# Four moves in the opening of a one-core attention and GEGLU block: the w_phi load, one x tile, the mask product and one PSUM copy

## The chip, the core and the metric

The kernel runs on one core of one Trainium2 chip. The metric is the device time of one execution in microseconds (us); the time of a version is the median of its runs. The names of the engines follow the profile: PE is TensorE's matmul, PEld its weight load, DVE is VectorE, ACT is ScalarE, POOL is GpSimd, SP is SyncE (here it only issues DMAs), and ACTq and SPq are the instruction queues of ACT and SP, from which DMAs are issued.

## What is computed

A pre-layernorm transformer block over 2048 rows of 640 features, in bf16: linear attention with a learned feature map (32 heads of 20), then a gated feed-forward layer of width 1536.

```python
def _A_ref(x, wqkv, w_phi, wo):
    qkv = (x @ wqkv).reshape(B, S, 3, H, Dh).transpose(2, 0, 3, 1, 4)
    q, k, v = qkv[0], qkv[1], qkv[2]
    pq = jnp.einsum("bhsd,hdf->bhsf", q, w_phi)
    pk = jnp.einsum("bhsd,hdf->bhsf", k, w_phi)
    phi_q = jnp.concatenate([_softmax(pq), _softmax(-pq)], axis=-1)
    phi_k = jnp.concatenate([_softmax(pk), _softmax(-pk)], axis=-1)
    kv = jnp.einsum("bhsf,bhsd->bhfd", phi_k, v)
    z  = jnp.einsum("bhsf->bhf", phi_k)
    num = jnp.einsum("bhqf,bhfd->bhqd", phi_q, kv)
    den = jnp.einsum("bhqf,bhf->bhq", phi_q, z)[..., None] + 1e-6
    return (num / den).transpose(0, 2, 1, 3).reshape(B, S, D) @ wo

def _B_ref(x, w_gate, w_up, w_down):
    return (_gelu(x @ w_gate) * (x @ w_up)) @ w_down

h = x + _A_ref(_layernorm(x), A_wqkv, A_w_phi, A_wo)
h2 = h + _B_ref(_layernorm(h), B_w_gate, B_w_up, B_w_down)
```

## The kernel before

**Tiling.** The 2048 rows are 16 tiles of 128 rows, in four blocks of four (x_sb[0] to x_sb[3]). The 640 features are 5 chunks of 128. Weights stay in SBUF.

**Stages.** (1) An opening, the first 17 us: loads, layernorm of the first six tiles, their transposes, the first V projections, and the fold of w_phi into W_k. (2) For each of 16 tiles a K projection, its exponentials, its normalisation, and the sums over rows (kv_tile). (3) Q projections and the attention output. (4) Gate, up and down projections for four blocks of rows. The change lies in stage 1.

**The fold.** w_phi acts on each head of 20 columns after the K projection. The kernel multiplies it into the weights instead: bd() (line 410) spreads w_phi (128 x 5 x 20) into a block-diagonal matrix BD (128 x 5 x 8 x 20, 800 elements in a partition) by a product with a 0/1 mask hmask, and fold() (line 224) multiplies the transposed W_k (WkT, loaded with transposing DMAs) by BD. A fold goes chunk by chunk, d = 0 to 4: six matmuls into a PSUM tile wa, then one copy of wa into Wk2. The tuple KA (line 48) names the chunks whose copy ACT makes; DVE makes the others. Before the change KA is (0, 1, 2, 4).

**Order.** The instructions of every engine are issued in the order in which the program is written, and each engine runs its own in that order, waiting at each for what it needs. The rows of lines 419 to 460 are that order for stage 1. What matters of it: the layernorm of tiles 0 and 1 is applied in two parts. The mean is subtracted before the transpose (xc, lines 263 and 403); the factor rstd is applied when V is copied out of PSUM (v_ev, line 306). For tile 0, ACT computes rstd. For tile 1, st_act (line 383) has ACT make the two sums and POOL make rstd, with lines 390 (variance plus epsilon), 391 (power -0.5) and 392 (its negative, used later by K). Tiles 2 and 3 have statistics on DVE (line 116, 120), the root on ACT (lines 126, 127) and the normalisation on DVE (ln_ap, line 151); tiles 4 and later have the root on POOL (lines 134, 135).

**PSUM.** All PSUM tiles of stage 1 come from one pool psG of four buffers. A new tile takes the buffer that was given back first, in the order of the program, and its first matmul waits for the copy that empties that buffer. In stage 1 the first fold's wa follows tile 0's V (pv), the second fold's wa follows tile 1's V, and the V projection of tile 3 follows the transpose of tile 3.

**Loads.** SP issues, in this order: x tiles 0, 1 and 2 (160 KB each), W_v's chunks 0 and 1, chunks 2 and 3 (320 KB each), x tile 3, W_v's chunk 4 (160 KB), x tiles 4 and 5 (320 KB), five transposing loads of W_k, and later the rest of x. ACT's queue issues w_phi (25 KB, in rows of 40 bytes), and then the load of an activation table (line 186).

Of the kernel before, what the change touches and what calls it, by code (L numbers as in the profile page):

```python
# [17 lines left out]
def kernel(  # L18
# [12 lines left out]
    nc = tc.nc  # L31
    P = 128
# [3 lines left out]
    Dh = 20  # L36
# [8 lines left out]
    H0 = [(P * c) // Dh for c in range(NC)]  # L45
    NH = [(P * c + P - 1) // Dh - H0[c] + 1 for c in range(NC)]
    VP = (0, 2, 4, 6, 9, 11)
    KA, QA = (0, 1, 2, 4), (0, 1, 2, 3, 4)
    LQ = (7, 8, 9, 9, 10)
    FQ = (10, 11, 12, 13, 14)  # L50

# [19 lines left out]
    x_v = A_x.rearrange("b (p t) d -> p (b t) d", t=NT)  # L71
    o_v = out.rearrange("b (p t) d -> p (b t) d", t=NT)
    w_v = A_wqkv.rearrange("(c p) n -> p c n", p=P)
    phi_v = A_w_phi.rearrange("h d f -> (h d) f")
# [8 lines left out]
    x_sb = [const.tile([P, 4, D], BF16, name=f"x_sb{b}") for b in range(NB)]  # L83
    wphi = const.tile([P, NC, Dh], BF16, name="wphi")
# [9 lines left out]
    BD = const.tile([P, NC, 8, Dh], BF16, name="BD")  # L94
# [86 lines left out]
    nc.gpsimd.memset(nhalf, -0.5)  # L181
    nc.gpsimd.memset(eps, EPS)
    nc.sync.dma_start(x_sb[0][:, 0:1, :], x_v[:, 0:1, :])
    nc.sync.dma_start(x_sb[0][:, 1:2, :], x_v[:, 1:2, :])
    nc.scalar.dma_start(wphi, phi_v.rearrange("(c p) f -> p c f", p=P))
    nc.scalar.add_instruction(mybir.InstLoadActFuncSet(name=nc.get_next_instruction_name(), act_func_set_id=6))
    nc.sync.dma_start(x_sb[0][:, 2:3, :], x_v[:, 2:3, :])
    nc.sync.dma_start(Wv[:, 0:2, :], w_v[:, 0:2, 2 * D:3 * D])
    nc.sync.dma_start(Wv[:, 2:4, :], w_v[:, 2:4, 2 * D:3 * D])
    nc.sync.dma_start(x_sb[0][:, 3:4, :], x_v[:, 3:4, :])  # L190
    nc.sync.dma_start(Wv[:, 4:5, :], w_v[:, 4:5, 2 * D:3 * D])
    nc.sync.dma_start(x_sb[1][:, 0:2, :], x_v[:, 4:6, :])

    def load_T(WT, i, *ds):
# [215 lines left out]
    def bd(c0, c1):  # L410

        n = c1 - c0
        nc.vector.tensor_tensor(BD[:, c0:c1], wphi[:, c0:c1, None, :].to_broadcast([P, n, 8, Dh]),
                                hmask[:, c0:c1, :, None].to_broadcast([P, n, 8, Dh]), ALU.mult)

    def tr_c(t):
# [6 lines left out]
    tr_c(1)  # L423
    ln_st(2, act=False, log=True)
    bd(0, NC)
    st_act(1, 1)
    warm(*[P] * 4)
# [430 lines left out]
```

## Time and profile before

| what | us |
|---|---|
| three runs | 275.83, 274.81, 275.75 |
| median | 275.75 |
| profiled execution, its own time | 275.48 |
| its span in the profile | 273.4 |
| PE busy (share of the span) | 268.0 (98%) |
| DVE, ACT, POOL busy | 174.5, 141.1, 96.0 |

The granted TensorE clock is 1.00 throughout. By stretches of the opening, from the busy time of each engine in given windows:

| window, us | PE | PEld | DVE | ACT | POOL | DMA share |
|---|---|---|---|---|---|---|
| 0 to 6 | 5.11 | 3.09 | 2.70 | 3.15 | 3.07 | 0.64 |
| 6 to 12 | 5.13 | 3.85 | 5.38 | 3.88 | 1.19 | 0.99 |
| 12 to 18 | 6.00 | 4.78 | 5.02 | 5.07 | 2.02 | 0.93 |
| 18 to 24 | 6.00 | 4.30 | 5.88 | 5.78 | 4.52 | 0.31 |

The first 4 us of PE are warm-up matmuls on constants (line 222), which produce nothing that is used. In a timeline row the numbers ahead of the engine are start and duration; the bracket behind a row gives how long the engine had been idle and what ended that. Rows on POOL are rough.

### The profile page before, as it was taken

How to read it: one execution, taken by the hardware profiler on the slowest of the kernel's cores; microseconds unless marked ns; L12 is line 12 of the kernel's file. 1: busy time of each engine (PE TensorE's matmuls, PEld its weight loads, DVE VectorE, ACT ScalarE, POOL GpSimd, SP SyncE). 2: the span in 40 equal slices, each digit the busy share in tenths (PEclk: the TensorE clock that was granted, in tenths of full speed). 3: DMA queues.
4: the chain of work that ended last, by engine and by line, in shares of the span. 5: the costliest groups of instructions: out<-in, count | busy, mean ns of one | idle time of the engine just before them, and what ended most of it. 6: DMA issues, size and time to landing. Idle time of an engine off the chain costs nothing.

```text
span 273.4 us, 7242 instructions
## 1 busy us (share of the span) xinstructions
PE 268.0 (98%) x2983; PEld 172.0 (63%) x3000; DVE 174.5 (64%) x332; ACT 141.1 (52%) x241; POOL 96.0 (35%) x220
## 2 busy tenths in 40 slices
PE   7999999999999999999999999999999999999996
PEld 4777767775555887788755555675555576444574
DVE  5889999997675866685459864336966333333332
ACT  5789897887799765364524445213354500223100
POOL 4248888775102226374221552101165300000000
PEclk9999999999999999999999999999999999999999
DMA  6972557670698022323202235210414111000011
GB/s 193 208 250 51 65 62 98 75 162 13 223 368 278 4 50 50 74 55 70 48 27 52 26 70 47 51 50 1 74 29 70 25 48 50 24 0 0 2 48 48
DMA packets 42400, 21.46 MB, mean 78 GB/s; under 512 B 35200, under 2 KB 40576, under 8 KB 42368
## 3 DMA queue, kind: packets, MB, share of 16 engines
q1 hardware_dynamic: 41712, 20.98, 33.9%
q8 instruction: 23, 0.38, 0.6%
q10 hardware_dynamic: 656, 0.03, 0.2%
q14 instruction: 9, 0.07, 0.1%
HBM read 10.18 MB, written 2.62 MB: 47 GB/s over the span
## 4 chain that ended last, share of the span: by engine, by line
PE 94%; DMA 3%; ACT 1%; issue 1%; DVE 1%; SPq 0%
PE gu L694 38%; PE pd L713 19%; PE po L634 8%; PE pq L376 8%; PE pk L287 7%; PE pv L287 6%; PE ab L562 2%; PE kvp L354 2%; DMA Wv<-in_A_wqkv_dram 2%; DMA LN1T<-ln 2%; PE wa L240 1%; PE tp L159 1%; PE pv L303 1%; ACT vS L307 1%; DVE LN1T L160 0%
## 5 line engine op out<-in xcount | busy, mean ns | idle before, releaser
L700 DVE TENSOR_TENSOR GT<-gu,g 128x512 bf16<-128x512 f32 (+1 forms) x60 | 34.5, 581 | 47.3 <-PE gu L694 38.5
L697 ACT ACTIVATE g<-gu 128x512 bf16<-128x512 f32 (+1 forms) x60 | 30.8, 513 | 63.5 <-PE gu L694 63.4
L694 PE MATMUL gu<-LN2T,Wg 128*128 128x512 bf16 (+1 forms) x289 | 61.2, 335 | 0.6
L694 PE MATMUL gu<-LN2T,Wu 128*128 128x512 bf16 (+1 forms) x300 | 61.8, 336 | 0.0
L713 PE MATMUL pd<-Wd,GT 128*128 128x320 bf16 (+2 forms) x396 | 53.5, 295 | 0.0
L713 PEld LDWEIGHTS <-GT 128*128 128x128 bf16 x396 | 37.9, 98 | 14.6 <-DVE GT L700 0.2
L694 PEld LDWEIGHTS <-Wu 128*128 128x128 bf16 x300 | 29.3, 98 | 22.6
L694 PEld LDWEIGHTS <-Wg 128*128 128x128 bf16 x300 | 28.6, 98 | 20.8
L287 PEld LDWEIGHTS <-LN1T 128*128 128x128 bf16 x290 | 27.7, 98 | 10.8 <-DMA LN1T<-ln 0.5
L716 DVE TENSOR_TENSOR y<-pd,x_sb 128x320 bf16<-128x320 f32 (+2 forms) x29 | 13.9, 480 | 29.4 <-PE pd L713 29.4
L335 POOL TENSOR_TENSOR vt<-vS,rs 128x672 bf16<-128x672 bf16 x22 | 29.2, 1346 | 8.6 <-DVE rs L331 7.9
L634 PE MATMUL po<-Wo,oT 128*128 128x320 bf16 x160 | 24.4, 299 | 0.0
L287 PE MATMUL pk<-Wk,LN1T 128*128 128x320 bf16 x160 | 24.2, 299 | 0.0
L376 PE MATMUL pq<-LN1T,Wq 128*128 128x512 bf16 x94 | 22.9, 379 | 0.3
L327 DVE TENSOR_REDUCE sk<-E 128x64 f32<-128x1280 bf16 x16 | 22.9, 1430 | 0.0
L381 ACT ACTIVATE Eq<-pq 128x1024 bf16<-128x1024 f32 (+1 forms) x26 | 20.0, 830 | 3.3 <-PE pq L376 3.3
L287 PE MATMUL pv<-Wv,LN1T 128*128 128x320 bf16 x130 | 19.8, 299 | 0.1
L320 ACT ACTIVATE E<-pk 128x640 bf16<-128x640 f32 x28 | 18.3, 708 | 3.2 <-PE pk L287 3.2
L634 PEld LDWEIGHTS <-oT 128*128 128x128 bf16 x160 | 15.5, 98 | 7.0 <-ACT oT L160 0.5
L146 ACT ACTIVATE ln<-x_sb,v,rstd 128x640 bf16<-128x640 bf16 x14 | 12.9, 923 | 10.7 <-POOL v L673 10.3
L611 DVE TENSOR_TENSOR tt<-AB,w 128x1280 bf16<-128x1280 f32 x12 | 17.8, 1485 | 1.0 <-POOL w L604 0.9
L376 PEld LDWEIGHTS <-Wq 128*128 128x128 bf16 x100 | 9.3, 98 | 9.7
(115 smaller groups left out, 289.2 us busy)
## 6 DMA issues: line engine op xcount, KB each, us to landing
out_dram<-y SPq DMA_DIRECT2D x15, 160.0 KB, 1.8
Wg<-in_B_w_gate_dram SPq DMA_DIRECT2D x1, 1920.0 KB, 7.8
Wu<-in_B_w_up_dram SPq DMA_DIRECT2D x1, 1920.0 KB, 8.8
Wd<-in_B_w_down_dram SPq DMA_DIRECT2D x2, 960.0 KB, 12.1
x_sb<-in_A_x_dram SPq DMA_DIRECT2D x2, 640.0 KB, 6.3
Wo<-in_A_wo_dram SPq DMA_DIRECT2D x1, 800.0 KB, 5.4
x_sb<-in_A_x_dram SPq DMA_DIRECT2D x4, 160.0 KB, 3.4
Wv<-in_A_wqkv_dram SPq DMA_DIRECT2D x2, 320.0 KB, 4.7
```

The source lines that it names most:

```text
L287: nc.tensor.matmul(ps[:, u, 0:HD], lhsT=lnT(t, c), rhs=W[:, c, u * HD:(u + 1) * HD], start=(c == 0), stop=(c == NC - 1))
L320: nc.scalar.activation(Ek[t][:, s, :].rearrange("p (u f) -> p u f", u=2), pk[:, :, 0:HD], ACTF.Exp, scale=((lnp[t][2], nrstd[t]) if t in C ...
L327: nc.vector.reduce_sum(sk, Ek[t].rearrange("p s (h f) -> p (s h) f", f=Dh), axis=AX.X)
L335: eng.tensor_tensor(vt[:, s], vS[t % 8], rs[:, s * H:(s + 1) * H, None].to_broadcast([P, H, VC]), ALU.mult)
L376: nc.tensor.matmul(pqs[j][:, i, :], lhsT=Wq2[:, kc, c * P:(c + 1) * P], rhs=LN1T[b][:, kc, :], start=(kc == 0), stop=(kc == NC - 1))
L381: nc.scalar.activation(Eq[j][:, :, s, :], pqs[j][:, 0:len(QG[j])], ACTF.Exp, scale=(1.0, -1.0)[s])
L611: nc.vector.tensor_tensor(tt.rearrange("p s (h f) -> p s h f", f=Dh), num, w[:, :, :, None].to_broadcast([P, 2, H, Dh]), ALU.mult)
L634: nc.tensor.matmul(pos[u], lhsT=st[t][:, c, :], rhs=Wo[:, c, u * HD:(u + 1) * HD], start=(c == 0), stop=(c == NC - 1))
L694: nc.tensor.matmul(gu[i][:, 0:n], lhsT=W[:, c, f * P:(f + 1) * P], rhs=LN2T[b][:, c, a0:a1], start=(c == 0), stop=(c == NC - 1))
L697: nc.scalar.activation(g[:, 0:n], gu[0][:, 0:n], ACTF.Gelu_apprx_tanh)
L700: nc.vector.tensor_tensor(st[b, "g", f][:, a0:a1], gu[1][:, 0:n], g[:, 0:n], ALU.mult)
L713: nc.tensor.matmul(ps, lhsT=st[b, "g", f][:, tl * P:(tl + 1) * P], rhs=Wd[:, f, f0:f1], start=(f == 0), stop=(f == NF - 1))
```

## The change

```diff
-    KA, QA = (0, 1, 2, 4), (0, 1, 2, 3, 4)
+    KA, QA = (1, 2, 4), (0, 1, 2, 3, 4)
...
     nc.sync.dma_start(x_sb[0][:, 0:1, :], x_v[:, 0:1, :])
-    nc.sync.dma_start(x_sb[0][:, 1:2, :], x_v[:, 1:2, :])
-    nc.scalar.dma_start(wphi, phi_v.rearrange("(c p) f -> p c f", p=P))
+    nc.scalar.dma_start(x_sb[0][:, 1:2, :], x_v[:, 1:2, :])
     nc.scalar.add_instruction(mybir.InstLoadActFuncSet(name=nc.get_next_instruction_name(), act_func_set_id=6))
     nc.sync.dma_start(x_sb[0][:, 2:3, :], x_v[:, 2:3, :])
     nc.sync.dma_start(Wv[:, 0:2, :], w_v[:, 0:2, 2 * D:3 * D])
     nc.sync.dma_start(Wv[:, 2:4, :], w_v[:, 2:4, 2 * D:3 * D])
     nc.sync.dma_start(x_sb[0][:, 3:4, :], x_v[:, 3:4, :])
     nc.sync.dma_start(Wv[:, 4:5, :], w_v[:, 4:5, 2 * D:3 * D])
+    nc.sync.dma_start(wphi, phi_v.rearrange("(c p) f -> p c f", p=P))
     nc.sync.dma_start(x_sb[1][:, 0:2, :], x_v[:, 4:6, :])
...
     def bd(c0, c1):
         n = c1 - c0
-        nc.vector.tensor_tensor(BD[:, c0:c1], wphi[:, c0:c1, None, :].to_broadcast([P, n, 8, Dh]),
+        nc.gpsimd.tensor_tensor(BD[:, c0:c1], wphi[:, c0:c1, None, :].to_broadcast([P, n, 8, Dh]),
                                 hmask[:, c0:c1, :, None].to_broadcast([P, n, 8, Dh]), ALU.mult)
```

w_phi's load goes from ACT's queue to SP's, behind the last chunk of W_v. x tile 1's load goes from SP's queue to ACT's, in the place that w_phi had. The mask product that makes BD runs on POOL instead of DVE; in the program's order it stands, as before, ahead of POOL's three instructions for rstd of tile 1. The copy of the first fold's PSUM tile runs on DVE instead of ACT. No work is added or taken out; the loop structure, the data types and the PSUM buffers are the same.

## The prediction

> **What bounds the kernel now.** I read the page first, then the chain of work in order of time, then the timeline of the first 20 us, then the DMA windows. The page says that PE is the bound.
>
> ```profile
> PE 268.0 (98%) x2983; PEld 172.0 (63%) x3000; DVE 174.5 (64%) x332; ACT 141.1 (52%) x241; POOL 96.0 (35%) x220
> ```
>
> PE is busy for 98% of the span, so the edits can only save where PE waits, and those places are few. The chain in order of time has, for the opening (start, duration, what):
>
> ```profile
> 2.18 4.55 DMA Wv<-in_A_wqkv_dram
> 6.73 0.04 issue
> 6.77 1.79 PE pv L303 x12
> ...
> 10.49 1.48 ACT vS L307 x2
> 11.96 0.04 issue
> 12.01 0.47 PE wa L240 x6
> 12.48 1.36 PE pv L287 x10
> ```
>
> The reader is to see two releases of PE: W_v's first half landing at 6.73, and tile 1's V copy (the second of the two vS) at 11.96, which frees the PSUM buffer for the second fold. From 12.01 PE runs without a break to 30 us and beyond, so whatever moves that 12.01 moves the end of the kernel, unless something behind takes over. The timeline shows how much slack stands around it:
>
> ```profile
> 6.77 1.79 PE L303 MATMUL pv<-Wv,LN1T 128*128 128x320 bf16 x12 [0.75 <-DMA Wv<-in_A_wqkv_dram]
> 6.90 0.95 DVE L413 TENSOR_TENSOR BD<-wphi,hmask 128x800 bf16<-128x800 bf16 x1
> 8.45 0.19 POOL L390 TENSOR_SCALAR va<-va 128x1 f32<-128x1 f32 x1 [2.46 <-ACT sqa L389]
> 8.72 0.57 POOL L391 TENSOR_TENSOR va<-va,nhalf 128x1 f32<-128x1 f32 x1
> 11.16 0.79 ACT L307 ACTIVATE vS<-pv,va 128x640 bf16<-128x640 f32 x1
> ```
>
> PE waited 0.75 us for W_v. POOL had rstd of tile 1 ready at 8.72 + 0.57 = 9.29; ACT used it at 11.16, so that side had 1.87 us to spare.
>
> **The loads.** On SP's queue x tile 1 drops out, so x tile 2, all of W_v and x tile 3 move up one issue slot, 0.45 to 0.51 us each (issues at 1.26, 1.71, 2.18, 2.66, 3.17, 3.68, by the timeline). w_phi takes the slot at 3.68, and x tiles 4 and 5 (4.16) and the W_k transposes (4.64) keep theirs. ACT's queue issues one DMA before and after (0.79), so the table load behind it is not touched. What w_phi cost where it stood is seen in the DMA window from 2.6 to 3.0 us:
>
> ```profile
> q10 hardware_dynamic: 601, 0.02, 103.0%
> q1 hardware_dynamic: 52, 0.05, 36.8%
> ```
>
> q10 is ACT's queue, q1 SP's: in 0.4 us w_phi's short packets took all 16 engines, while the x and W_v stream had a third. So the first half of W_v gains one slot (0.47) or that stretch (0.4), not both: the queue is full from 4.5 us on, and I take 0.45. It lands at 6.73 - 0.45 = 6.28. Bounds: 0, if the stream was held by something else, and 0.72, since the transposed tile 0 that the same matmul reads was ready only at about 6.05 (ACT's copies start at 5.36, two in 1.29). x tile 1 now shares the engines with x tile 0: 160 KB each, so tile 0 may land up to 160 KB later, at the 304 GB/s of the window from 2.2 to 2.6 us 0.5 us, and at best not at all, as w_phi stood beside it before. I take 0.15; the 0.23 us between 6.05 and 6.28 hide it, and without that cover it would come off the gain one for one. x tile 1 itself, at 4.03 before, lands at least its slot of 0.47 earlier, but tile 1's chain waits for DVE and ACT behind tile 0, so this is worth nothing.
>
> So PE's start gains 0.45, and without any other limit the second fold starts at 12.01 - 0.47 = 11.54 (0.45 plus what little of the release wait goes).
>
> **The mask product.** DVE loses 0.95 us at 6.90. DVE was there only waiting for ACT's root of tile 2 (ready at 7.54, ln at 7.76), so this frees about 0.2 us on the chain, and keeps tile 2 and 3 abreast of the earlier PE. On POOL the product takes longer. The nearest rows are the other broadcast products of the same form:
>
> ```profile
> L335 POOL TENSOR_TENSOR vt<-vS,rs x22: 1305/1313/1966, 22.5 to 66.1; 128x672 bf16<-128x672 bf16 x22
> L335 DVE TENSOR_TENSOR vt<-vS,rs x10: 841/914/1754, 27.3 to 66.1; 128x672 bf16<-128x672 bf16 x10
> ```
>
> 1.313 x 800/672 = 1.56 us. Bounds: DVE's own 0.95 below, 1.966 x 800/672 = 2.34 above. I take 1.56, as the median and the minimum of 22 agree. The Trainium skill's page GPSIMD Engine Reference (section Engine selection) speaks against this edit: it says two-input elementwise work is about twice as slow on GpSimd and belongs on VectorE. By it the product would take 2 x 0.946 = 1.89 (an estimate from that page's ratio), and the sum below would end at +0.10 instead of -0.23; the rows here give 1.313/0.841 = 1.56 times.
>
> **When it can start.** It needs w_phi, which now lands behind W_v. The sum of work ahead of it in the queue is the same as was ahead of W_v's last chunk, which was issued in the same slot at 3.68:
>
> ```profile
> Wv<-in_A_wqkv_dram SPq DMA_DIRECT2D x1, 160.0 KB, 4.7
> ...
> wphi<-in_A_w_phi_dram ACTq DMA_DIRECT2D x1, 25.0 KB, 2.8
> ```
>
> So it lands at 3.68 + 4.7 = 8.38. Bounds: 3.68 + 2.8 = 6.48, its own time from an empty queue, and 9.84, when the first W_k transpose behind it lands (4.64 + 5.2). I take 8.38, for the queue is full then (share 102% from 7.5 to 8.0 us).
>
> **Who waits.** Behind the product on POOL stand lines 390, 391 and 392 for tile 1, and behind those lines 134 and 135 for tile 4. ACT waits for 391 with v_ev(1), and queued behind that on ACT are v_ev(2) and all later copies; PE waits with the second fold. Before, line 390 to rstd took 9.29 - 8.45 = 0.84, v_ev(1) to the fold's start 12.01 - 11.16 = 0.85, and a handover between engines costs 0.02 to 0.05 (the "issue" pieces of the chain, 0.04 before the fold at 12.01); I count 0.05, three times. So the second fold starts at landing + 0.05 + product + 0.05 + 0.84 + 0.05 + 0.85 = landing + product + 1.84 = 8.38 + 1.56 + 1.84 = 11.78. That is later than the 11.54 that PE could do, so POOL is what decides, and the gain is 12.01 - 11.78 = **0.23 us**. Landing plus product must be under 10.17 us for any gain at all. BD itself is there at 9.99, a microsecond before the first fold (11.41 - 0.45 = 10.96) reads it.
>
> **The first fold's copy.** ACT loses 0.69 us right behind v_ev(1), so v_ev(2) follows at once and ACT stays ahead. DVE gains 0.82 (its row for the copy of the fourth fold), after its copy of tile 3's transpose at about 11.7. DVE stood idle there for 0.19 and 0.69 us (before ln of tile 4, and before the copy of tile 4's transpose at 14.47). Tile 4's ln moves to about 12.95 to 13.4, and PE transposes it at 13.99 - 0.23 = 13.76, so the copy costs nothing; with that cover gone it would cost up to 0.82 - 0.19 = 0.63, by tile 4's transpose. The third fold takes this buffer at 13.4, long after the copy's end near 12.5.
>
> **Sum.** Loads -0.45 and product on POOL +0.22 leave -0.23. Further on, tile 6's statistics (15.96 before) meet their x, issued in an unchanged slot 11.64 and landing 4.1 us later at 15.74: 0.22 us of room, just enough. The wait of 0.47 us for a transposed tile at 36.4 follows ACT's work and so moves with PE. The profiled execution goes from 275.48 (span 273.4, and 2.1 around it) to 275.25. The median of the runs, 275.75, is 0.27 above it; against it the forecast is 275.75 - 0.23 = 275.5.
>
> **The rivals.**
>
> *The product is late* (the other side: slower). One mechanism: w_phi's 640 short packets land late or the product runs long, and POOL's rstd for tile 1 holds v_ev(1), hence the second fold. It decides from landing + product = 10.17. With the first transpose's 5.2 us, 3.68 + 5.2 = 8.88, and 2.34 for the product, the fold starts at 13.06: +1.05, 276.8. At the far bounds, 9.84 + 2.34 + 1.84 = 14.02: +2.0, 277.8. For it: 0.23 us is a thin margin, and a DVE product of the same form went from 0.84 to 1.75 where it stood beside POOL's, so these two can block each other: from 10.15 us DVE wants to normalise tile 3, and would be held to the product's end if that came later. The Trainium skill's page SBUF — State Buffer (section Who interferes with whom) has this as an exclusive lock for a whole instruction; the 1.75 us agrees. Against: w_phi's packets moved in 0.4 us when the engines were free for them, and POOL's durations are steady.
>
> *The product is early.* If w_phi's short packets overtake the stream as they did from 2.6 to 3.0, landing + product stays under 9.9 and PE's own pace decides: -0.47, 275.3. Against it: one queue now holds both.
>
> *The loads do not move.* If the engines and not the issue slots set W_v's landing, and x tile 1 takes from x tile 0 what w_phi took, PE starts at 6.77 as before. The chain through POOL is then shorter than PE's own and the fold starts at 12.01: 0.0, 275.75. For it: x tile 2 took 4.1 us from its issue, while the queue was only 60% to 75% busy from 3.6 to 4.5, so something else than volume held it.
>
> **How the numbers follow.** Forecast 42%, late 28%, early 14%, loads unmoved 16%. What a measurement can tell from no change is about 0.5%, 1.4 us. Only the late case reaches it upward, and half of it does: 14% slower. The early case would have to remove the wait at 36.4 as well and some more, so 7% is what I leave for faster; 79% stays within. The range runs from the early case less 0.7 us for the spread of the runs (274.81 to 275.83 before), 274.6, to the late case's 276.8 and a little over, 277.0.
>
> **What would show it.** In the changed profile: the first V matmul (line 303) starts near 6.3, with a shorter wait for W_v; line 413 stands on POOL from about 8.4 for 1.5 to 1.6 us; line 391 ends near 10.9; ACT's vS of tile 1 starts near 10.9, with POOL as its releaser; the second fold starts near 11.8 and PE's rows behind it lie 0.2 us earlier. Wrong would be: line 413 ending after 10.2; ln of tile 3 held beside it; the copy on DVE making tile 4's transpose late; or the 0.2 us lost again at 15.9 or at 36.4.

## The result, and the profile after

| | kernel before | changed kernel |
|---|---|---|
| median of 22 runs, us | 275.27 (274.59 to 276.72) | 275.93 (275.27 to 277.52) |
| ratio, 95% interval | | 1.0032 [1.002, 1.0044] |
| profiled execution, us | 275.48 | 276.00 |
| its span, us | 273.4 | 274.2 |

The changed kernel is 0.3% slower, less than the 0.5% that the prediction took as the bound of what can be told, but with an interval that leaves out both no change and the forecast gain. Its 22 times are not one heap: 15 lie from 275.27 to 276.24 (median 275.72) and 7 from 276.9 to 277.5. Of the kernel before, 21 of 22 lie at 275.83 or less and one at 276.72. So there are two things to explain: a shift of 0.45 us in the lower group (275.72 against 275.27), and an upper group some 1.3 us above it. Two runs further down, one of wphi_act_late at 283.89 us and one of the kernel before at 465.34 us, had a granted clock of 0.95 and 0.56 and are left out of the ratios and counts.

The page of the changed kernel says that PE bounds it as before:

```profile
PE 267.8 (98%) x2983; PEld 171.6 (63%) x3000; DVE 173.8 (63%) x332; ACT 140.3 (51%) x240; POOL 97.7 (36%) x221
```

Its chain of waits in order of time (start, duration, what) opens differently. Before, it began with W_v's landing; now it begins with x tile 0:

```profile
0.79 3.12 DMA x_sb<-in_A_x_dram
3.94 0.90 DVE statsc L116 x2
...
6.04 0.70 ACT LN1T L160
6.79 1.85 PE pv L303 x12
...
10.56 1.47 ACT vS L307 x2
12.08 0.47 PE wa L240 x6
```

The first row of the next fence is of the kernel before, the others are the timeline rows of the changed kernel that answer to those shown of before:

```profile
3.26 0.89 DVE L116 BATCH_NORM_STATS2 statsc<-x_sb 128x6 f32<-128x320 bf16 x2 [1.20 <-DMA x_sb<-in_A_x_dram]
3.94 0.89 DVE L116 BATCH_NORM_STATS2 statsc<-x_sb 128x6 f32<-128x320 bf16 x2 [1.89 <-DMA x_sb<-in_A_x_dram]
5.55 0.75 PE L159 MATMUL tp<-ident,xc 128*128 128x128 bf16 x10 [1.23 <-DVE xc L264]
6.79 1.85 PE L303 MATMUL pv<-Wv,LN1T 128*128 128x320 bf16 x12 [0.26 <-ACT LN1T L160]
8.28 1.53 POOL L413 TENSOR_TENSOR BD<-wphi,hmask 128x800 bf16<-128x800 bf16 x1 [1.88 <-DMA wphi<-in_A_w_phi_dram]
10.17 0.57 POOL L391 TENSOR_TENSOR va<-va,nhalf 128x1 f32<-128x1 f32 x1
11.24 0.79 ACT L307 ACTIVATE vS<-pv,va 128x640 bf16<-128x640 f32 x1
12.09 0.81 DVE L251 CAST Wk<-wa 128x640 bf16<-128x640 f32 x1
```

The statistics of tile 0 start at 3.94; before, at 3.26. The first V matmul starts at 6.79 (6.77 before), and the bracket names ACT's copy of the transposed tile 0, no longer W_v. W_v did come earlier, but what it is multiplied with came later. Line 413 stands where it was forecast, POOL is done with line 391 at 10.74, and ACT reads that only at 11.24, so POOL holds nobody. The second fold starts at 12.08 (12.01 before) and the first K matmul at 16.74 (16.66).

Why x tile 0 is late can be read in the DMA windows. From 1.8 to 2.2 us the changed kernel shows (queue, packets, MB, share of 16 engines), where q10 is ACT's queue with x tile 1 and q1 is SP's with x tile 0:

```profile
q10 hardware_dynamic: 36, 0.05, 82.5%
q1 hardware_dynamic: 2, 0.00, 1.7%
```

Kernel before, same window; w_phi on ACT's queue has moved nothing yet:

```profile
q1 hardware_dynamic: 21, 0.03, 55.3%
```

The two tiles were issued at the same time, 0.79 us, and here ACT's queue had the first packets. That order is not what makes x tile 0 late. In x1_alone, an experiment below with the same two loads side by side, SP's queue had the first packets, and the statistics of tile 0 still start at 3.88. Its window from 1.8 to 2.2 us:

```profile
q1 hardware_dynamic: 24, 0.03, 65.3%
q10 hardware_dynamic: 3, 0.00, 2.6%
```

What such traces have in common is the window from 2.2 to 2.6 us, first the kernel before, then the changed kernel:

```profile
DMA packets 128, 0.12 MB, mean 304 GB/s; under 512 B 34, under 2 KB 128, under 8 KB 128
DMA packets 52, 0.07 MB, mean 166 GB/s; under 512 B 0, under 2 KB 52, under 8 KB 52
```

With the two x tiles on two queues the engines moved 166 GB/s there (154 in x1_alone, 141 in after_again), with them on one queue 304 (326 in x1_on_sp). From 2.6 to 3.0 us the two queues moved about the same amount, 68 packets and 58, and the tiles of the changed kernel landed 0.2 us apart, at 3.72 and 3.92. So the two tiles did share the engines, and from 2.2 to 2.6 us the pair of queues moved only about half as much as one. Why it did is not known.

More is lost behind the opening. The chain of the changed kernel from 24 to 39 us:

```profile
24.57 3.47 DMA LN1T<-ln
28.08 1.53 PE pv L287 x10
...
33.14 4.31 DMA LN1T<-ln
37.50 1.53 PE pv L287 x10
```

These are the V projections of tiles 8 and 11, each waiting for a transposing transfer. Before, they started at 27.53 and 36.86. The waits stand in PEld's rows, first of the kernel before (tile 11), then of the changed kernel (tiles 8 and 11):

```profile
36.85 1.20 PEld L287 LDWEIGHTS <-LN1T 128*128 128x128 bf16 x10 [0.47 <-DMA LN1T<-ln]
```

```profile
28.08 2.56 PEld L287 LDWEIGHTS <-LN1T 128*128 128x128 bf16 x20 [0.65 <-DMA LN1T<-ln]
37.49 1.20 PEld L287 LDWEIGHTS <-LN1T 128*128 128x128 bf16 x10 [0.42 <-DMA LN1T<-ln]
```

The wait for tile 11 is about as long as before; the one for tile 8 is new. Its transfer took 3.47 us, against 2.6 before. From the V of tile 11 to the end of the span it is 236.6 us before and 236.7 after, so of the 0.8 us that the span grew, 0.08 lie ahead of the first K matmul, 0.56 between it and the V of tile 11 (0.47 of them up to the V of tile 8), and 0.1 behind. I call the middle part **the stretch**: 20.20 us before, 20.76 after.

### The profile page after: what moved, and what is told of

It reads as the page before. It is cut to its first block, busy times and chain, and to the rows that moved or that the text cites. A ratio compares the mean times of both kernels' runs of the same rounds, so it can differ in the third digit from the quotient of the medians.

```text
span 274.2 us, 7242 instructions
## 1 busy us (share of the span) xinstructions
PE 267.8 (98%) x2983; PEld 171.6 (63%) x3000; DVE 173.8 (63%) x332; ACT 140.3 (51%) x240; POOL 97.7 (36%) x221
## 4 chain that ended last, share of the span: by engine, by line
PE 89%; DMA 4%; DVE 4%; ACT 2%; issue 1%; POOL 0%; POOLq 0%
PE gu L694 38%; PE pd L713 19%; PE po L634 8%; PE pq L376 8%; PE pk L287 4%; PE pv L287 4%; DMA LN1T<-ln 3%; PE ab L562 2%; PE kvp L354 2%; DMA x_sb<-in_A_x_dram 1%; DVE stats L116 1%; PE wa L240 1%; PE tp L159 1%; PE pv L303 1%; ACT vS L307 1%
## 5 line engine op out<-in xcount | busy, mean ns | idle before, releaser
L694 PEld LDWEIGHTS <-Wg 128*128 128x128 bf16 x300 | 28.6, 98 | 20.8
```

The lines of the kernel that those rows point to most:

```text
L694: nc.tensor.matmul(gu[i][:, 0:n], lhsT=W[:, c, f * P:(f + 1) * P], rhs=LN2T[b][:, c, a0:a1], start=(c == 0), stop=(c == NC - 1))
```

## The experiments

All ratios are against the kernel before, run beside them. Each has 12 runs, but for after_x67 (9), x1_on_sp_x67 (6) and after_warm (4). The columns behind the ratio come from one profiled execution each.

| run | ratio [95%] | first V | first K | stretch | what the stretch shows |
|---|---|---|---|---|---|
| x1_on_sp | 1.0007 [0.9992, 1.0022] | 5.97 | 16.29 | 20.93 | DVE waits 0.87 for x |
| x1_alone | 1.0004 [0.9988, 1.0021] | 6.73 | 16.68 | 20.04 | |
| after_again | 1.0032 [1.0013, 1.005] | 6.87 | 16.82 | 21.05 | DVE waits 0.84 for x |
| before_again | 0.9996 [0.9978, 1.0014] | 6.57 | 16.45 | 20.16 | |
| ka_back | 1.0035 [1.0019, 1.0051] | 6.95 | 16.90 | 20.80 | DVE waits 0.70 for x |
| wphi_on_act | 1.0032 [1.0017, 1.0047] | 6.99 | 16.95 | 20.86 | late fetch |
| wphi_act_late | 1.0008 [0.9995, 1.0021] | 6.33 | 16.22 | 21.09 | DVE waits 0.84 for x |
| wphi_twice | 1.0006 [0.9995, 1.0018] | 6.61 | 16.50 | 20.37 | |
| bd_pool | 0.9996 [0.9983, 1.0009] | 6.65 | 16.54 | 20.71 | late fetch |
| before_x67 | 0.9994 [0.9978, 1.0011] | 6.49 | 16.38 | 20.12 | |
| after_x67 | 1.0058 [1.0031, 1.0085] | 6.96 | | | W_k transpose late |
| x1_on_sp_x67 | 1.0074 [1.0055, 1.0093] | 6.22 | | | W_k transpose late |
| after_eps | 1.0031 [1.001, 1.0052] | 7.16 | 18.04 | 19.89 | |
| pool_plus1 | 1.0006 [0.9985, 1.0027] | 6.60 | 16.48 | 21.16 | DVE waits 1.23 for x |
| x1_on_sp_eps | 1.0011 [0.9993, 1.0028] | 6.37 | 16.52 | 20.72 | DVE waits 0.36 for x |
| wphi_act_late_eps | 1.0007 [0.9987, 1.0027] | 6.87 | 16.76 | 19.96 | |
| after_warm | 1.0154 [1.0137, 1.0171] | 6.78 | 17.54 | 21.54 | fetches beside tile 8's transfer |
| before_gap | 1.0012 [0.9991, 1.0033] | 6.39 | 17.98 | 20.11 | |

"DVE waits for x" is its wait for x tiles 6 and 7 ahead of tile 6's statistics. "Late fetch" is the first transfer on queue q14 (an instruction fetch by the profile's name) behind the opening, at 26 to 28 us instead of near 18.

### Where x tile 1 is loaded

x1_on_sp is the changed kernel with x tile 1 back on SP's queue; x1_alone is the kernel before with x tile 1 alone moved.

```diff
# x1_on_sp, against the changed kernel
-    nc.scalar.dma_start(x_sb[0][:, 1:2, :], x_v[:, 1:2, :])
+    nc.sync.dma_start(x_sb[0][:, 1:2, :], x_v[:, 1:2, :])
# x1_alone, against the kernel before
-    nc.sync.dma_start(x_sb[0][:, 1:2, :], x_v[:, 1:2, :])
+    nc.scalar.dma_start(x_sb[0][:, 1:2, :], x_v[:, 1:2, :])
```

> The changed kernel with x tile 1 alone put back on SP's queue, behind x tile 0. Theory 1 (x tile 1, first on the wire from ACT's queue, holds up x tile 0, which landed at 3.94 instead of 3.26 and so took back what W_v gained): DVE's first statistics start at 3.2 to 3.3, the first V matmul at 6.2 to 6.4 instead of 6.79, and the second fold is then bound by POOL (w_phi issued one slot later, landing near 8.7, rstd of tile 1 near 11.1): 11.9 to 12.0. Time 0 to 0.3 us under before, 0.6 or more under the changed kernel. Rival (the product on POOL and the copy on DVE cost the time, the loads do not): first V matmul wherever it may be, second fold at 12.1 or later, time as the changed kernel, +0.3% on before.

> The kernel before with x tile 1 alone moved to ACT's queue, ahead of w_phi; the mask product stays on DVE and the copies as before. Theory 1: DVE's first statistics start at 3.8 to 4.0, the first V matmul at 6.8 to 7.0, time 0.1 to 0.7 us over before. Rival (product and copy cost the time): first statistics may be late, but the time is that of before within 0.1% or less than it.

In the opening it went the way that was expected, with everything a little earlier than the expected numbers. With x tile 1 on SP the statistics of tile 0 start at 3.12 and the first V at 5.97; with x tile 1 alone moved they start at 3.88 and 6.73. In x1_on_sp POOL also decides the second fold, as the prediction had it. Its timeline:

```profile
5.97 1.85 PE L303 MATMUL pv<-Wv,LN1T 128*128 128x320 bf16 x12 [0.25 <-ACT LN1T L160]
10.79 0.80 ACT L307 ACTIVATE vS<-pv,va 128x640 bf16<-128x640 f32 x1 [0.26 <-POOL va L391]
11.63 0.47 PE L240 MATMUL wa<-BD,WkT 128*128 128x140 bf16 x6 [0.49 <-ACT vS L307]
16.54 0.89 DVE L116 BATCH_NORM_STATS2 stats<-x_sb 128x6 f32<-128x320 bf16 x2 [0.87 <-DMA x_sb<-in_A_x_dram]
```

The brackets are the reading: ACT waits for POOL's line 391, PE for ACT. But the 0.4 us won up to there did not reach the end. The last row shows DVE standing 0.87 us for x tiles 6 and 7, whose load took 4.7 us from its issue here and 4.1 before, and the V of tile 11 starts at 37.22, later than before's 36.86. The time is that of before, not below it. That of x1_alone is too (1.0004), where 0.1 to 0.7 us more was expected; the interval allows most of that range.

### Repeats, and the copy

after_again and before_again are the two kernels unaltered; ka_back gives the first fold's copy back to ACT.

```diff
# ka_back, against the changed kernel
-    KA, QA = (1, 2, 4), (0, 1, 2, 3, 4)
+    KA, QA = (0, 1, 2, 4), (0, 1, 2, 3, 4)
```

> The changed kernel once more, for a second profile. Theory 2 (the half microsecond at 28 us, where PE waits for the transposed tile 8, comes from a late transposing DMA that falls together with an instruction fetch, and belongs to the execution, not to the edits): the opening repeats within 0.1 us (first V matmul 6.8, second fold 12.1), while the waits for transposed tiles at 28 and 37 us come out different, by 0.3 us or more in at least one. Rival (it belongs to the program): both waits return at 28 and 37 us with 0.3 to 0.6 us each.

> The kernel before once more, for a second profile and a second set of times. Theory 2: opening within 0.1 us (6.8 and 12.0), the wait for a transposed tile at 36.4 comes out different or another one appears. Rival: the same single wait of 0.5 us at 36.4 and none at 27.5. Time against before within 0.1%.

> The changed kernel with the copy of the first fold back on ACT. Theory 3: ACT stands 0.69 longer behind tile 1's V, the second fold is as late as with the change (12.0 to 12.2), time as the changed kernel within 0.1% (+0.2 to +0.4% on before). Rival (the copy on DVE delays DVE's packed queue, and that is the loss): DVE's statistics of tiles 8 and 9 start earlier and the time falls to within 0.1% of before.

The loss came back the same (1.0032), and giving the copy back to ACT changed nothing (1.0035): the copy on DVE is cleared.

The waits did not come back. In after_again PE does not wait for tile 8 at all, and the wait for tile 11 is longer:

```profile
37.87 1.20 PEld L287 LDWEIGHTS <-LN1T 128*128 128x128 bf16 x10 [1.15 <-DMA LN1T<-ln]
```

So the same program loses its half microsecond at different places in two executions; the edits do not fix the place. The kernel before, in before_again, has the same single wait as in its first profile, 0.40 us at 36.6, but its opening is 0.2 us earlier (first K at 16.45 against 16.66), where 0.1 was expected at most. So much an opening differs between executions of one program; the change was forecast to move it by 0.23.

### Loading x tiles 6 and 7 earlier

The first theory of the stretch was that x tiles 6 and 7 are issued too late. Their load moved ahead of the last two W_k transposes, in three kernels.

```diff
# after_x67, x1_on_sp_x67, before_x67
-    load_T(WkT, 1, *range(NC))
+    load_T(WkT, 1, 0, 1, 2)
+    nc.sync.dma_start(x_sb[1][:, 2:4, :], x_v[:, 6:8, :])
+    load_T(WkT, 1, 3, 4)
...
-    nc.sync.dma_start(x_sb[1][:, 2:4, :], x_v[:, 6:8, :])
```

> The changed kernel, with the load of x tiles 6 and 7 issued behind the third W_k transpose on SP instead of behind the fifth. Theory 3 (the rest of the loss, and the runs near 277 us, come from x tiles 6 and 7 landing late: DVE then stands at their statistics, its packed queue runs late up to tile 11's ln, and PE waits for tile 11's transposed DMA near 37 us): DVE no longer waits at tile 6's statistics, the first V matmul of tile 11 starts 20.0 to 20.3 us after the first K matmul instead of 20.8 to 21.1, no run above 276.7, time within 0.1% of before. Rival (the product on POOL or the copy on DVE cost it): +0.3% stays.

> The changed kernel with x tile 1 back on SP's queue and the load of tiles 6 and 7 behind the third W_k transpose. Theories 1 and 3 together: first K matmul at 16.2 to 16.4 as with x tile 1 on SP alone, V of tile 11 at 20.0 to 20.3 us behind it, time 0.3 to 0.5 us under before (0.9983), the fastest so far. Rival: the gain of the opening is swallowed again near 37 us and the time is that of before.

> The kernel before with only the load of tiles 6 and 7 behind the third W_k transpose: the control. Theory 3: the opening unchanged (first V matmul 6.6 to 6.8), the time as before or up to 0.2 us less, and no run above 276.6. Rival (the earlier load helps by itself, whatever the change did): 0.5 us or more under before.

It made the two changed kernels worse and left the kernel before as it was. The chain of x1_on_sp_x67 has the transfer that then decides, the fifth W_k transpose, and PE's waits have what it cost (total, times, longest):

```profile
11.07 5.24 DMA WkT<-in_A_wqkv_dram
```

```profile
PE wa L242 <- DMA WkT<-in_A_wqkv_dram: 1.7, 1, 1.7
```

The theory fell as a remedy: on one queue, what is put ahead delays what stands behind.

### Where w_phi is loaded, and the product alone

wphi_twice loads w_phi a second time into a tile that nothing reads, in the kernel before; wphi_on_act gives w_phi back to ACT's queue behind x tile 1; wphi_act_late puts it behind the table load, with x tile 1 on SP; bd_pool is the kernel before with the product alone on POOL.

```diff
# wphi_twice, against the kernel before
     nc.sync.dma_start(Wv[:, 4:5, :], w_v[:, 4:5, 2 * D:3 * D])
+    nc.sync.dma_start(wphi2, phi_v.rearrange("(c p) f -> p c f", p=P))
# wphi_on_act, against the changed kernel
     nc.scalar.dma_start(x_sb[0][:, 1:2, :], x_v[:, 1:2, :])
+    nc.scalar.dma_start(wphi, phi_v.rearrange("(c p) f -> p c f", p=P))
...
-    nc.sync.dma_start(wphi, phi_v.rearrange("(c p) f -> p c f", p=P))
# wphi_act_late, against the changed kernel
-    nc.scalar.dma_start(x_sb[0][:, 1:2, :], x_v[:, 1:2, :])
+    nc.sync.dma_start(x_sb[0][:, 1:2, :], x_v[:, 1:2, :])
     nc.scalar.add_instruction(mybir.InstLoadActFuncSet(name=nc.get_next_instruction_name(), act_func_set_id=6))
+    nc.scalar.dma_start(wphi, phi_v.rearrange("(c p) f -> p c f", p=P))
...
-    nc.sync.dma_start(wphi, phi_v.rearrange("(c p) f -> p c f", p=P))
# bd_pool, against the kernel before
-        nc.vector.tensor_tensor(BD[:, c0:c1], wphi[:, c0:c1, None, :].to_broadcast([P, n, 8, Dh]),
+        nc.gpsimd.tensor_tensor(BD[:, c0:c1], wphi[:, c0:c1, None, :].to_broadcast([P, n, 8, Dh]),
```

> The kernel before with a second load of w_phi, into a tile that nothing reads, on SP's queue behind W_v's last chunk; nothing else moved. Theory 4 (w_phi's 640 short packets on SP's queue stop SP from issuing: the W_k transposes behind them are issued 0.3 to 1 us later, so the load of tiles 6 and 7 goes out at 11.9 to 12.4 instead of 11.5 to 11.6, lands after 16.3, and DVE's packed queue runs late up to tile 11): that load at 11.9 or later, a DVE wait of 0.3 us or more at tile 6's statistics, V of tile 11 at 20.6 to 21.1 us behind the first K matmul, time +0.2 to +0.5% on before. Rival (the product on POOL and what it does to the engines' instruction fetches cost the time): SP's issues and the time as before within 0.1%.

> The changed kernel with w_phi alone back on ACT's queue, behind x tile 1; product on POOL and copy on DVE as changed. Theory 4: the load of tiles 6 and 7 goes out at 11.5 to 11.7, no DVE wait at tile 6, time within 0.1% of before although the first V matmul is still at 6.7 to 6.9. Rival (product and copy): +0.2 to +0.4% as the changed kernel.

> The changed kernel with x tile 1 back on SP's queue and w_phi on ACT's queue behind the table load: neither of the two suspects is left. Theories 1 and 4: first statistics at 3.1 to 3.3, first V matmul at 6.0 to 6.3, the product on POOL done by 9.3 so that it holds nothing, first K matmul at 16.0 to 16.3, time 0.3 to 0.5 us under before. Rival: the gain of the opening is swallowed near 37 us again, and the time is that of before or above.

> The kernel before with the mask product alone on POOL; w_phi still loaded first on ACT's queue. Theory 4: the product runs from about 3.9 for 1.5 us with nothing waiting for it, opening within 0.2 us of before or earlier, time within 0.1% of before or under it. Rival (product on POOL costs the time): +0.2% or more.

w_phi's place on SP's queue does not matter (1.0006 for a second copy there, 1.0032 with it taken away). wphi_act_late had the early opening that was expected of it (first K at 16.22), but not the 0.3 to 0.5 us under before: its ratio is 1.0008. The product alone on POOL costs nothing in the median (0.9996). Put together with x1_alone this gives a square: x tile 1 moved alone 1.0004, product moved alone 0.9996, both moved 1.0031 to 1.0035 in five sets of runs (the changed kernel twice, ka_back, wphi_on_act and after_eps). By the medians neither edit is at fault alone; but the interval of x1_alone reaches up to 1.0021, so a part of the loss could still be its own.

### The instruction fetch

In the traces so far with the product on POOL the first q14 fetch came at 26 to 28 us, beside the transposing transfers of tiles 8 and 9 (at 30 in after_x67, which ran some 4 us late by then); with the product on DVE, near 18. The changed kernel has it in its DMA window from 26 to 28 us; in that of the kernel before there is only q1:

```profile
q1 hardware_dynamic: 493, 0.12, 31.1%
q14 instruction: 1, 0.01, 1.0%
```

The second theory was that one instruction more on POOL moves this fetch. Three kernels take POOL's memset of eps away, and pool_plus1 adds one memset to the kernel before.

```diff
# after_eps, x1_on_sp_eps, wphi_act_late_eps
-    nc.gpsimd.memset(eps, EPS)
+    nc.vector.memset(eps, EPS)
# pool_plus1, against the kernel before
+    nc.gpsimd.memset(pad, 0.0)
```

> The changed kernel with the memset of eps on VectorE in place of GpSimd, so that GpSimd issues as many instructions as before the change, with the mask product still on it. Fetch theory (one more GpSimd instruction moves an instruction fetch onto the transposing transfer of tile 8): the first fetch behind the opening is back near 18 us, the stretch from the first K matmul to the V of tile 11 is 20.0 to 20.4 us, and the time is within 0.1% of before (first K matmul 16.7 to 16.9, as in the changed kernel). Rival (the product's own work on GpSimd): the fetch stays wherever it is, the stretch is 20.7 to 21.1 us and the time 0.3% above before.

> The kernel before with one memset more on GpSimd, of a tile of 128x1 that nothing reads. Fetch theory: the first fetch behind the opening comes at 26 to 28 us, the stretch from the first K matmul to the V of tile 11 is 20.7 to 21.1 us in place of 20.0 to 20.4, and the time 0.1 to 0.3% above before. Rival (the product's work): the fetch near 18 us, the stretch as before, the time as before within 0.1%.

> The changed kernel with x tile 1 back on SyncE's queue and the memset of eps on VectorE. Fetch theory: first K matmul at 16.2 to 16.4 us, stretch to the V of tile 11 20.0 to 20.4 us, so 0.2 to 0.5 us under before (ratio 0.998 to 0.9993). Rival (the product's work on GpSimd): the stretch is 20.7 to 21.1 us and the time that of before (ratio 0.9995 to 1.001).

> The changed kernel with x tile 1 back on SyncE's queue, w_phi on ScalarE's queue behind the load of the table, and the memset of eps on VectorE. Fetch theory: first K matmul at 16.2 to 16.4 us, stretch 20.0 to 20.4 us, 0.2 to 0.5 us under before (ratio 0.998 to 0.9993). Rival: stretch 20.7 to 21.1 us, the time that of before (ratio 0.9995 to 1.001).

The fetch did go back to 18 or 19 us in all three, and in after_eps and wphi_act_late_eps the stretch was 19.89 and 19.96, the product still on POOL. That much speaks for the theory. But the times did not follow: 1.0031, 1.0011 and 1.0007 against 1.0032, 1.0007 and 1.0008 without the edit. And in pool_plus1 one instruction more did not move the fetch (19.2 us), yet its stretch was the longest of these four. The timeline of pool_plus1 says why:

```profile
17.09 0.89 DVE L117 BATCH_NORM_STATS2 stats<-x_sb 128x6 f32<-128x320 bf16 x2 [1.23 <-DMA x_sb<-in_A_x_dram]
```

So over 17 traces, the two kernels' own among them (all but after_x67, x1_on_sp_x67 and after_warm), a long stretch, 20.7 or more, goes with one of two things, DVE's wait for x tiles 6 and 7 or a late fetch, and a short one with neither; where the product is computed does not decide it. What brings on either was not found.

Two more things stand in the traces. DVE's wait goes with the time that the load of x tiles 6 and 7 took from its issue: 4.3 to 5.5 us in the six of these traces with the wait, 3.4 to 4.2 in the ten others that issue it at its old place. It differs between executions of one program, 3.7 in the changed kernel and 4.9 in after_again. And a fetch beside a transposing transfer is no single coincidence. All 20 traces together give the landing of 198 transposing transfers of normalised tiles. A fetch begins 0.5 to 2.2 us behind the issue of 53 of them, and 52 of these 53 took 3.1 to 4.9 us; of the other 145, 128 took less than 2.7. Both the new wait at tile 8 and the old one at tile 11 are of that kind: fetches begin at 26.7 us in the changed kernel, 2.1 us behind the issue of tile 8's transfer, and at 33.6 and 33.7 in the kernel before, 1.0 and 1.1 behind that of tile 11. That slow transfers and fetches go together is shown by this; that the fetch makes the transfer slow is likely, but no run moved a fetch alone.

after_eps showed something else. Its time lay in the upper group (7 of 12 runs at 276.78 or more, the profiled one 276.87), its stretch was short, and its first K matmul came at 18.04. PE's rows of its opening:

```profile
5.66 1.25 PE L159 MATMUL tp<-ident,xc 128*128 128x128 bf16 x10 [0.83 <-DVE xc L264]
6.70 0.63 PE L220 MATMUL wu<-const-bfloat16-1.0 128*128 128x128 bf16 x4
7.16 2.79 PE L303 MATMUL pv<-Wv,LN1T 128*128 128x320 bf16 x12
10.06 2.61 PE L303 MATMUL pv<-Wv,LN1T 128*128 128x320 bf16 x18
```

Ten transposes in 1.25 us; the changed kernel's profile has the same ten in 0.75. Twelve V matmuls in 2.79, against 1.85. Matmul by matmul, the first V starts follow each other at 267 ns until 9.2 us, then at 136: TensorE ran at half its rate until then. In the changed kernel's own trace the rate doubles at 3.6 us, within the warm-up matmuls, in after_again at 6.1. The column of the granted clock shows 1.00 throughout, so it is the rows, not that column, that tell it. Everything that stands before the doubling costs double, and the later x tile 0 leaves PE standing 0.5 to 1.5 us between its warm-up and its first transposes in all kernels with x tile 1 on ACT's queue (at most 0.46 with it on SP's), as long as the warm-up is not altered. Such a stop does not cost the time in every execution: the changed kernel's trace has one of 1.23 us, and in it the rate had doubled before.

The Trainium skill, page TensorE: Matmul & The Clock Gate (Part 1: The HAM clock gate), says that the array runs at half rate until a free-running window of about 3.4 us was busy, so that the point of change varies from run to run. The 267 and 136 ns here agree with the half rate. The points, from 3.6 to 9.2 us, lie much further apart than the 500 ns to either side that the page gives for matmuls in an unbroken row; here PE stood still in between. The window itself no run here shows.

### Filling the stop, and making one

after_warm adds eight warm-up matmuls of 128 columns to the changed kernel; before_gap takes eight from the kernel before.

```diff
# after_warm, against the changed kernel
-    warm(*[512] * 5, 256, *[P] * 14)
+    warm(*[512] * 5, 256, *[P] * 22)
# before_gap, against the kernel before
-    warm(*[512] * 5, 256, *[P] * 14)
+    warm(*[512] * 5, 256, *[P] * 6)
```

> The changed kernel with eight more warm-up matmuls of 128 columns, which fill 0.45 us (at full rate) to 0.86 us (at half rate) of TensorE's stop of 0.5 to 1.5 us ahead of the first transposes. Theory (the stop makes TensorE reach its full rate later in some runs, which costs up to 1.3 us in the first V matmuls): runs of 276.6 us and more fall from 4 in 10 to at most 2 in 12, and the median lies at 275.5 to 276.0 us, 0.0 to 0.15% above before, the rest being the loss behind the opening. Rival (the whole loss lies behind the opening, where an instruction fetch or a late x tile holds the transposing transfers): 4 in 10 stay and the ratio is 1.003.

> The kernel before with eight warm-up matmuls of 128 columns fewer, so that TensorE stops for 0.5 to 0.9 us ahead of its first transposes; everything else is as before. Theory (the stop): 3 to 6 runs in 12 at 276.6 us or more, median 0.1 to 0.4% above before. Rival (behind the opening): time as before within 0.1%.

before_gap shows the mechanism by itself. PE's rows:

```profile
4.90 1.25 PE L159 MATMUL tp<-ident,xc 128*128 128x128 bf16 x10 [0.92 <-DVE xc L264]
6.39 3.38 PE L303 MATMUL pv<-Wv,LN1T 128*128 128x320 bf16 x12
17.98 1.25 PE L287 MATMUL pk<-Wk,LN1T 128*128 128x320 bf16 x8
```

With no edit but fewer warm-up matmuls, PE stood 0.92 us, the first twelve V matmuls took 3.38 us instead of 1.79, and the first K matmul came at 17.98 instead of 16.66. The 12 times fall apart: three from 274.51 to 274.88, nine from 275.84 to 276.65. The count that was expected, 3 to 6 at 276.6 or more, was missed (2), because both groups lie lower than I had put them; the ratio, 1.0012, is as expected, but its interval reaches below 1. The edit also makes the busy time ahead of the stop shorter, so stop and warm-up are not told apart.

after_warm failed as a test. Four runs, 279.38 to 280.13: the stop was filled and the V matmuls ran at full rate (first V at 6.78), but other waits appeared further on. Two rows of its chain show slow transposing transfers:

```profile
10.70 4.83 DMA WkT<-in_A_wqkv_dram
...
25.37 4.63 DMA LN1T<-ln
```

and its DMA window from 26 to 28 us, where two fetches fall together:

```profile
q1 hardware_dynamic: 519, 0.13, 97.0%
q14 instruction: 1, 0.01, 3.9%
q8 instruction: 1, 0.02, 3.4%
```

Before, the window holds no fetch and q1 takes 27.2% for 435 packets; here 97% for 519. These transfers are less than half of the loss. Of the 3.8 us by which the span is longer than the changed kernel's (278.0 against 274.2), 0.8 lie ahead of the first K matmul, 0.8 in the stretch and 2.2 behind it. There PE stands twice for 1.0 us, at 67 and at 137 us, in places where the changed kernel's list of waits has nothing:

```profile
PE pd L713 <- DVE GT L700: 1.0, 1, 1.0
PE pq L376 <- issue: 1.0, 1, 1.0
```

Eight more matmuls at 4 us changed waits as far on as 137 us, and the ratio went to 1.0154. What makes the two late stops is not known; that the fetches make the early ones is argued.

## Why the prediction was right or wrong

**W_v's landing (gain 0.45): right, and cancelled.** V no longer waits for W_v. In after_eps and ka_back, which load as the changed kernel does, W_v's first half landed at 6.22 and 6.44 against 6.73, a gain of 0.5 and 0.3.

**x tile 0 (late by 0.15, at most 0.5): the step that failed first.** It was 0.68, outside its bounds. That the two tiles share the engines was right; the size was not. The bound of 0.5 set 160 KB against the 304 GB/s of one queue, and with two queues the same window moved 166. The rest of the sum then follows: the transposed tile 0, put at 6.05, comes 0.68 later at 6.73, and the first V started at 6.79. The cover of 0.23 us that the prediction named was used up and the 0.45 with it. With this step put right, in x1_on_sp, most of the loss went: 1.0007 against 1.0032, and none of 12 runs at 276.6 or more. But the forecast gain did not come with it. The opening was won there (second fold at 11.63, against 11.78 forecast), and the time was still that of before, for the reasons given below under tile 6 and the wait at 36.4.

**The product and POOL's chain: right in size, not binding.** Forecast: landing at 8.38, product 1.56, line 391 done near 10.9. Measured: 8.2, 1.53, 10.74. In x1_on_sp, where it does decide, the formula (landing + product + 1.84) gives 8.12 + 1.53 + 1.84 = 11.49, and the fold started at 11.63. The ratio to DVE's 0.95 is 1.6, not the 2 cited from the Trainium skill's page GPSIMD Engine Reference (section Engine selection). The lock cited from the Trainium skill's page SBUF — State Buffer (section Who interferes with whom) was not put to the test: from 8.28 to 9.81 DVE ran only statistics, which read one tile, and a copy out of PSUM, and these kept their 0.49 us.

**The copy on DVE (nothing): right**, by ka_back.

**Tile 6's statistics (0.22 us of room, "just enough"): wrong in some runs.** The sum took the load of x tiles 6 and 7 as 4.1 us, as before; it took 3.7 to 4.9. No wait in the profile of the changed kernel, 0.84 us in that of its repeat, and 0.36 to 0.87 in both kernels with x tile 1 on SP and w_phi on SP's queue.

**The wait at 36.4 ("moves with PE"): right in the profile of the changed kernel (0.42 us against 0.47), wrong in its repeat (1.15).** What the sum did not have is that transposing transfers differ in length from one execution to the next: in the changed kernel's profile tile 8's took 3.47 us in place of 2.6 and made a wait of its own. In both profiles the stretch grew, from 20.2 to 20.8 and 21.05. This accounts for the lower group's shift, as far as one profile of each shows, and for x1_on_sp keeping nothing of its early opening. Why the fetches and the landing of x tiles 6 and 7 fall otherwise is open.

**What was not in the sum: TensorE's rate.** The sum moved PE's rows with their durations. A stop ahead of the first transposes can go with doubled durations, and the prediction's own delay of x tile 0 would have lengthened such a stop. The upper group is this, as far as shown: after_eps has it in a trace with x tile 1 on ACT's queue and before_gap by making a stop. In the five sets of runs with both edits 28 of 70 are at 276.6 or more, in the five with the product on POOL and x tile 1 on SP's queue 5 of 59, in the runs of the kernel before beside them all 11 of 169. x1_alone, with a stop of 0.66 us in its profile, has 2 of 12: too few to say whether the product is needed for it. No run of the changed kernel itself from the upper group was profiled.

The forecast of 275.5 was 0.4 us low, and the result lies in the range and within 0.5% of before. That it came so near is in part luck: it started from the median of three runs, 275.75, and 22 runs of the kernel before give 275.27. As a change, -0.23 us was forecast and +0.66 measured. The mechanism that was forecast to set the end, POOL's product, existed, but not in the lead. Of the rivals, the unmoved loads name the right place, a second fold at 12.0, and half of the reason: x tile 1 did take from x tile 0, but W_v's landing did move. No variant beats the kernel before: the lowest ratios, before_x67 and bd_pool, have 1 within their intervals.

## What to carry to other kernels

A second queue does not make two loads faster: here two tiles of 160 KB on two queues landed together, 0.5 us or more later than the first of them when both stood on one queue. Let the load that starts the critical chain go alone. Ahead of the first matmuls, ask not only when their data come but how long TensorE stands before it: two executions with a stop of 0.8 to 0.9 us (after_eps and before_gap) ran their first matmuls at half rate and reached the first K matmul 1.3 us late. A few tenths won in an opening are worth nothing if the next stage waits for transfers with their own times, and then look at the list of times before the median: two groups need two explanations.

## What the runs showed of the hardware that was not expected

- Two loads of 160 KB issued together from two queues: the engines moved 166 GB/s from 2.2 to 2.6 us, against 304 with both on one queue, and in the changed kernel the tiles landed 0.2 us apart. Which queue had the first packets changed from trace to trace (36 against 2 for ACT's in the changed kernel, 24 against 3 for SP's in x1_alone).
- TensorE's doubling of rate, at 3.6, 6.1 and 9.2 us in two traces of the changed kernel and one of after_eps, with the granted clock at 1.00 in all of them.
- Instruction fetches are transfers on the same engines. Of 53 transposing transfers with a fetch in them 52 took 3.1 to 4.9 us, of 145 without one 128 took less than 2.7.
- Eight more matmuls in the opening made the span 3.8 us longer, 2.2 of them more than 39 us into the kernel, with two stops of TensorE of 1.0 us.
